# A third SBUF place for the down weights of a mixture-of-experts kernel, with router weights and list rows moved

## The chip, the cores and the metric

One core of one Trainium2 chip runs the whole kernel. The metric is the device time of one execution in microseconds (us); less is better. The kernel before took 942.89 us, the median of three runs (942.83 to 943.75). All times inside the kernel come from one profiled execution, and times of day in it are counted from its first instruction.

## The reference

The output mixes two branches by a sigmoid gate for each of 2048 tokens of 512 numbers. Branch A is a long causal convolution: a 4-tap convolution of `k` times `v`, then an FFT convolution with `ssm_k`, times `q`. Branch B is a mixture of eight experts with two chosen for each token:

```python
logits = einsum("bsd,de->bse", x, w_router)            # x = A_q, 8 experts
topk_idx = argsort(logits)[..., -2:]; gates = softmax(take(logits, topk_idx))
hg = silu(einsum("bsd,edf->bsef", x, w_gate))          # D = 512, F = 1376
hu = einsum("bsd,edf->bsef", x, w_up)
y  = einsum("bsef,efd->bsed", hg * hu, w_down)         # weighted by the gates and summed
g  = sigmoid((x * gate_w).sum(-1))
out = g * A(q, k, v) + (1 - g) * B(x)
```

## The kernel before

The kernel computes only the chosen tokens of each expert. It first finds the router's logits on TensorE (PE), ranks them, starts the fullest expert from a short list made for it alone, and makes the lists of all other experts (`routing`, `places`, `read_lists`) while the first expert runs. Then the experts r = 0 to 7 follow one another, each with up to 568 tokens.

**An expert.** F = 1376 is cut into eleven tiles ft = 0 to 10. For each, `up(ft)` loads the gate and up weights (`raw`, three places in SBUF, line 573) and the down weights (`rd`, line 623; for ft 2 of the first expert line 620), splits each into a high and a low fp32r half (`gh` on ScalarE, line 584, and `gl` on VectorE, line 590; `dh` on ScalarE, line 651, and `dl` on VectorE, line 653), and multiplies: the tokens are cut into two halves h, and for each h a product g and a product u of twelve matmuls (lines 200 to 202) fill a PSUM bank each, of three banks in turn. ScalarE makes `sg` = silu(g) (line 642), VectorE multiplies it by u (line 643), and the result is split into `hh` (ScalarE, 644) and `hl` (VectorE, 645). After ft 2, 5, 8 and 10 a group of tiles goes through the down product (`down`, tiles `yp`, gathered in `ya` on lines 678 and 680 or 701 and 704). The five places of `dh` and `dl` come free in groups of three when a down product is done, so the next three `rd` are wanted close together.

**Waits by place.** A load into a tile waits until the last reader of the tile that held its place before is done. With two places for `rd`, `rd` of ft 2 waits for `dl` of ft 0, and so on. The sync engine's queue (SP) issues loads strictly in order, so a load that waits holds back all loads behind it. Pools have named tags: `R3 = (3, 2, 2, 2)` on line 46 gives the number of places of `raw`, `gh`, `gl` and `rd`.

**The order of work.** Up to the first products of expert 0 the order is written by hand (`manual_schedule`). After that a list scheduler with a simulated clock places every instruction on its engine, so that a change of places can move instructions anywhere; each engine then runs its own list in order. Pieces of branch A are mixed in by `tick`: the spectra of `ssm_k` (`ks`, lines 279 and 293, with `kr` loaded on 224), the tap convolution `x_stage1` (`krow`, `v`, `tmp`, `acc`, lines 361 to 365), `x_stage2` and `y_stage`. The loads of the first expert that are not in the hand-written part wait for a gather to end (`behind_rows`, tied to the split of the last gathered rows on line 522).

**The parts that move.** `wr` (lines 153 and 154) holds the router weights and two small tables, 265 numbers per partition; only the start reads it. `late` holds two constant rows for the lists and a dummy column, loaded before expert 0; `idf` and `wsum` are working rows of `read_lists`, which runs once, at ft 5 of expert 0 (lines 913 to 918). All four lie in the pool `consts`, which lives as long as the kernel. The pool `route` ends when expert 0 has its rows. The tag "T" (three places of 512 numbers) serves `dD`, then `v` and `tmp` of `x_stage1`. `dD` is added to one row of `kr` by GpSimd (line 321).

Of the kernel before, what the change touches and what calls it, by code (L numbers as in the profile page):

```python
# [12 lines left out]
F32 = mybir.dt.float32  # L13
# [11 lines left out]
P = 128  # L25
S = 2048
D = 512
KT = D // P
F = 1376
E = 8  # L30
# [9 lines left out]
NT = MAIN + OVER  # L40
# [2 lines left out]
FT = [(i * P, min(P, F - i * P)) for i in range((F + P - 1) // P)]  # L43
SPREAD = 0.97
BW, EV, FX = (5, 3, 2)
R3 = (3, 2, 2, 2)
G0 = 5
TM = (5, 6, 7)
QA = 2
# [84 lines left out]
NLATE = P + 2 * NT + 1  # L134
# [4 lines left out]
def gated_mix(ctx: ExitStack, tc: tile.TileContext, a, out):  # L139
    nc = tc.nc  # L140
    sync, act, dve, pool, pe = nc.sync, nc.scalar, nc.vector, nc.gpsimd, nc.tensor

    dram = ctx.enter_context(tc.tile_pool(name="dram", bufs=1, space=DRAM))
    cp = ctx.enter_context(tc.tile_pool(name="consts", bufs=1))
# [5 lines left out]
    zd = dram.tile([P, 2, PL, D], F32, name="zd")  # L150
    lst = dram.tile([P, OVER, 2], I32, name="lst")

    wr = cp.tile([P, KT * 32 + 2 * E * E + E + 1], F32, name="wr")
    sync.dma_start(wr, a["wr"])
    ident = cp.tile([P, P], F32, name="ident")
    G = cp.tile([P, PL], F32, name="G")
    sidx = cp.tile([P, NT], I32, name="sidx")
# [4 lines left out]
    rc = cp.tile([P, NROW], F32, name="rc")  # L162
    colf = cp.tile([P, 2, PL], F32, name="colf")
    pay = cp.tile([P, 3, 2, PL], F32R, name="pay")
    idf = cp.tile([P, NT], F32, name="idf")
    wsum = cp.tile([P, NT], F32, name="wsum")
    late = cp.tile([P, 2 * NT + 1], F32, name="late")
    cols, spare, dummy = late[:, :NT], late[:, NT:2 * NT], late[:, 2 * NT:]
    row = cp.tile([P, 2, PL], F32, name="row")
    blk = cp.tile([P, OVER], I32, name="blk")  # L170
    nblk = cp.tile([P, 1], I32, name="nblk")
# [14 lines left out]
    def t2k(tag, bufs, name, dt=F32):  # L186
        return fp.tile([P, D], dt, tag=tag, bufs=bufs, name=name)
# [124 lines left out]
    def k_load(pl):  # L312
        n = k_order.index(pl)
        if n % 2 == 0:
            kr["two"] = two("B", f"kr{pl}")
        kr[pl] = half(kr["two"], n % 2)
        fetch(kr[pl], rows(a["ssk"], pl))
        if pl == 0:
            dD = t2k("T", 3, "dD")[0:1, :]
            sync.dma_start(dD, a["ssd"])  # L320
            pool.tensor_add(kr[0][0:1, :], kr[0][0:1, :], dD)
# [229 lines left out]
    def expert(r):  # L551
# [12 lines left out]
        def load(ft, eng=sync):  # L564
            fw = FT[ft][1]
            raw = wp.tile([P, 2 * KT * P], F32, tag="raw", bufs=R3[0], name=f"raw{r}_{ft}")
            n = 2 * KT * fw
# [11 lines left out]
        def split(ft, *engines, halves=(0, 1)):  # L579
            raw = st["raw", ft]  # L580
            n = raw.shape[1]
            if act in engines:
                st["gh", ft] = wp.tile([P, 2 * KT * P], F32R, tag="gh", bufs=R3[1], name=f"gh{r}_{ft}")[:, :n]
                anchor[f"gh {r} {ft}"] = act.activation(st["gh", ft], raw, AF.Copy).ins  # L584
            if dve in engines:
                if ("gl", ft) not in st:
                    st["gl", ft] = wp.tile([P, 2 * KT * P], F32R, tag="gl", bufs=R3[2], name=f"gl{r}_{ft}")[:, :n]
                c = slice(halves[0] * n // 2, (halves[-1] + 1) * n // 2)
# [26 lines left out]
        def load_down(ft, eng=sync):  # L615
            f0, fw = FT[ft]
            rd = wp.tile([P, D], F32, tag="rd", bufs=R3[3], name=f"rd{r}_{ft}")
            src = a["wd"][ds(st["e"], 1), f0:f0 + fw, :].rearrange("o f d -> (o f) d")
# [113 lines left out]
    wp = mp_ctx.enter_context(tc.tile_pool(name="moe_in", bufs=1))  # L732
    early = ExitStack()
    rp = early.enter_context(tc.tile_pool(name="route", bufs=1))
    io8 = rc[:, :8]
    capv = rc[:, 8:16]
    m_le = rc[:, 16:80].rearrange("p (a b) -> p a b", a=E)
# [35 lines left out]
    k_load(k_order[2])  # L773
    k_load(k_order[3])
    k_load(k_order[4])
    sync.dma_start(late, a["c_small"][:, P:NLATE])
    sync.dma_start(ident, a["c_small"][:, :P])
    for n in range(5, SEQ_N):
        k_load(k_order[n])
# [151 lines left out]
    for i in range(4):  # L931
        dve.tensor_tensor(hot0[:, i], u0[:, 4 * i:4 * i + 4].unsqueeze(1).to_broadcast([P, P, 4]), io4, op=ALU.is_equal)
        for j in range(4):
            n = 4 * i + j
# [200 lines left out]
    with tc.For_i(0, nb_v, 1) as b:  # L1135
        with tc.tile_pool(name="over", bufs=1) as op:
# [15 lines left out]
            for ft, (f0, fw) in enumerate(FT):  # L1152
                n = 2 * KT * fw
# [68 lines left out]
```

## Time and profile before

| | |
|---|---|
| median of three runs | 942.89 us (942.83 to 943.75) |
| the profiled execution | 943.57 us |
| its span, first to last instruction | 941.3 us |
| PE busy | 923.5 us, 98% of the span |
| VectorE (DVE) busy | 633.6 us, 67% |
| ScalarE (ACT) busy | 509.7 us, 54% |
| GpSimd (POOL) busy | 146.6 us, 16% |
| mean granted TensorE clock | 0.998 |
| DMA | 172.02 MB, mean 183 GB/s |

The profile counts an engine as busy while one of its instructions runs. A wait of one engine costs time only where PE, the engine that is nearly always busy, stands still for it, or at the two ends of the span. The views used below are the page, busy time by stretches, the list of who waited for whom, the DMA view of a stretch, and the order of instructions by time. In the last, each row has the start, the duration, engine, line, operation, the tile written and the tiles read, and in brackets the idle time just before with what ended it.

### The profile page before, as it was taken

To read this page: it belongs to the slowest core of one execution; us is meant where nothing else is said; L and a number is where in the kernel's file an instruction comes from. 1 tells how busy PE (TensorE), PEld (TensorE's weight loads), DVE (VectorE), ACT (ScalarE), POOL (GpSimd) and SP (SyncE) were. 2 spreads that over 40 slices of the span, in tenths; PEclk is the share of its full clock that TensorE was granted. 3 is DMA by queue.
4 is the path that set the end of the run, shared out by engine and by line. 5 is a ranking of instruction groups with operands and counts; after the bars stand their busy time and mean duration, and the time that the engine had idled before them with its cause. 6 is when DMAs were issued, how large, how long until landed. Compare 5 with 4: busy or idle time off the path is not lost. (4 is left out here: it accounts for less than half of the span.)

```text
span 941.3 us, 18097 instructions
## 1 busy us (share of the span) xinstructions
PE 923.5 (98%) x6957; PEld 830.0 (88%) x6957; DVE 633.6 (67%) x1131; ACT 509.7 (54%) x883; POOL 146.6 (16%) x137
## 2 busy tenths in 40 slices
PE   8999999999999999999999999999999999999996
PEld 4679999999999999978898889888887989889984
DVE  4796699999996557556767666765777645554541
ACT  4654334755456546478656876668766544234330
POOL 0320210300003020131101211013010310121012
PEclk9999999999999999999999999999999999999999
DMA  9895945754456463456445655456553786787233
GB/s 329 301 349 220 376 153 191 207 193 155 140 202 183 157 205 122 135 135 204 144 136 169 166 181 175 141 167 174 182 172 121 188 276 181 193 200 217 70 54 45
DMA packets 76378, 172.02 MB, mean 183 GB/s; under 512 B 8481, under 2 KB 9377, under 8 KB 76162
## 3 DMA queue, kind: packets, MB, share of 16 engines
q1 hardware_dynamic: 53490, 121.89, 38.4%
q0 software_dynamic: 12464, 29.02, 13.6%
q10 hardware_dynamic: 10336, 19.93, 5.8%
q8 instruction: 56, 0.92, 0.4%
q14 instruction: 32, 0.26, 0.1%
HBM read 127.24 MB, written 43.57 MB: 181 GB/s over the span
## 5 line engine op out<-in xcount | busy, mean ns | idle before, releaser
L200 PE MATMUL u<-xh,gh 128*128 128x256 f32 (+14 forms) x704 | 202.0, 287 | 2.5 <-ACT sg L642 2.5
L200 PE MATMUL g<-xh,gh 128*128 128x256 f32 (+17 forms) x696 | 200.8, 288 | 1.9 <-DVE sg L643 1.9
L202 PE MATMUL u<-xh,gl 128*128 128x256 f32 (+14 forms) x704 | 201.3, 286 | 0.0
L201 PE MATMUL u<-xl,gh 128*128 128x256 f32 (+14 forms) x704 | 201.1, 286 | 0.0
L202 PE MATMUL g<-xh,gl 128*128 128x256 f32 (+17 forms) x696 | 198.8, 286 | 0.0
L201 PE MATMUL g<-xl,gh 128*128 128x256 f32 (+17 forms) x696 | 198.6, 285 | 0.0
L200 PEld LDWEIGHTS g<-xh,gh 128*128 128x128 f32 (+1 forms) x696 | 129.5, 186 | 8.8 <-DVE sg L643 4.5
L200 PEld LDWEIGHTS u<-xh,gh 128*128 128x128 f32 (+1 forms) x704 | 130.9, 186 | 5.9 <-ACT sg L642 3.1
L201 PEld LDWEIGHTS u<-xl,gh 128*128 128x128 f32 (+1 forms) x704 | 130.9, 186 | 4.3 <-issue 4.1
L202 PEld LDWEIGHTS g<-xh,gl 128*128 128x128 f32 (+1 forms) x696 | 129.6, 186 | 4.3 <-issue 4.1
L202 PEld LDWEIGHTS u<-xh,gl 128*128 128x128 f32 (+1 forms) x704 | 131.1, 186 | 0.9 <-issue 0.8
L201 PEld LDWEIGHTS g<-xl,gh 128*128 128x128 f32 (+1 forms) x696 | 129.5, 186 | 2.4 <-issue 0.8
L642 ACT ACTIVATE sg<-g 128x256 f32<-128x256 f32 (+14 forms) x176 | 68.0, 387 | 111.9 <-PE g L202 110.6
L200 PE MATMUL yp<-hh,dh 128*128 128x264 f32 (+13 forms) x440 | 127.1, 290 | 0.0
L202 PE MATMUL yp<-hh,dl 128*128 128x264 f32 (+13 forms) x440 | 126.8, 289 | 0.0
L201 PE MATMUL yp<-hl,dh 128*128 128x264 f32 (+13 forms) x440 | 126.8, 288 | 0.0
L644 ACT ACTIVATE hh<-sg 128x256 fp32r<-128x256 f32 (+14 forms) x176 | 73.1, 418 | 98.6 <-DVE sg L643 98.0
L643 DVE TENSOR_TENSOR sg<-sg,u 128x256 f32<-128x256 f32 (+14 forms) x176 | 74.8, 426 | 72.2 <-PE u L202 70.7
L584 ACT ACTIVATE gh<-raw 128x1024 fp32r<-128x1024 f32 (+1 forms) x88 | 91.4, 1038 | 50.8 <-PE u L201 50.0
L590 DVE TENSOR_TENSOR gl<-raw,gh 128x1024 fp32r<-128x1024 f32 (+1 forms) x88 | 105.3, 1197 | 18.6 <-ACT gh L584 17.8
L645 DVE TENSOR_TENSOR hl<-sg,hh 128x256 fp32r<-128x256 f32 (+14 forms) x176 | 75.0, 429 | 24.8 <-ACT hh L644 24.5
L653 DVE TENSOR_TENSOR dl<-rd,dh 128x512 fp32r<-128x512 f32 (+1 forms) x88 | 59.5, 685 | 39.8 <-ACT dh L651 39.7
(283 smaller groups left out, 1549.6 us busy)
## 6 DMA issues: line engine op xcount, KB each, us to landing
raw<-in_wgu SPq DMA_DIRECT2D x80, 512.0 KB, 4.4
rd<-in_wd SPq DMA_DIRECT2D x80, 256.0 KB, 4.3
kl<-kd SPq DMA_DIRECT2D x16, 512.0 KB, 5.2
xl<-xd SPq DMA_DIRECT2D x32, 256.0 KB, 4.1
zd<-ze ACTq DMA_DIRECT2D x16, 512.0 KB, 3.9
zl<-zd SPq DMA_DIRECT2D x16, 512.0 KB, 5.9
out<-zt SPq DMA_DIRECT2D x21, 256.0 KB, 6.1
krow<-in_kpad SPq DMA_DIRECT2D x19, 256.0 KB, 5.5
```

What stands on the lines that cost most here:

```text
L200: pe.matmul(p, wh, hi, start=start, stop=False)
L201: pe.matmul(p, wh, lo, start=False, stop=False)
L202: return pe.matmul(p, wl, hi, start=False, stop=stop)
L584: anchor[f"gh {r} {ft}"] = act.activation(st["gh", ft], raw, AF.Copy).ins
L590: dve.tensor_sub(st["gl", ft][:, c], raw[:, c], st["gh", ft][:, c].bitcast(F32))
L642: act.activation(sg[:fw, :nn], pp[0][:fw, :nn], AF.Silu)
L643: dve.tensor_mul(sg[:fw, :nn], sg[:fw, :nn], pp[1][:fw, :nn])
L644: act.activation(hh[:fw, sl], sg[:fw, :nn], AF.Copy)
L645: dve.tensor_sub(hl[:fw, sl], sg[:fw, :nn], hh[:fw, sl].bitcast(F32))
L653: dve.tensor_sub(dl[:fw], rd[:fw], dh[:fw].bitcast(F32))
```

## The change

`rd` gets three places instead of two. Room for it comes from the pool `consts`: `wr` moves into the pool `route`, and `late`, `idf` and `wsum` become five slices of one tile that takes the first turn of the tag "T".

```diff
-R3 = (3, 2, 2, 2)
+R3 = (3, 2, 2, 3)
...
-    wr = cp.tile([P, KT * 32 + 2 * E * E + E + 1], F32, name="wr")
-    sync.dma_start(wr, a["wr"])
...
-    idf = cp.tile([P, NT], F32, name="idf")
-    wsum = cp.tile([P, NT], F32, name="wsum")
-    late = cp.tile([P, 2 * NT + 1], F32, name="late")
-    cols, spare, dummy = late[:, :NT], late[:, NT:2 * NT], late[:, 2 * NT:]
...
     rp = early.enter_context(tc.tile_pool(name="route", bufs=1))
+    wr = rp.tile([P, KT * 32 + 2 * E * E + E + 1], F32, name="wr")
+    sync.dma_start(wr, a["wr"])
+    late = t2k("T", 3, "late")
+    cols, spare, dummy, idf, wsum = (late[:, o:o + n] for o, n in ((0, NT), (NT, NT), (2 * NT, 1), (2 * NT + 1, NT), (3 * NT + 1, NT)))
...
-    sync.dma_start(late, a["c_small"][:, P:NLATE])
+    sync.dma_start(late[:, :2 * NT + 1], a["c_small"][:, P:NLATE])
```

Line numbers of the changed kernel are six lower from line 169 to 734 and two lower from line 735 on. What the scheduler makes of it is shown at three places. In the names, `dh_2` is `dh` of ft 2, `sg_1_0` is `sg` of ft 1, half 0; the last number of a name is the program's own count.

**First expert, ScalarE, ft 0 to 1.** Before:

```order
L642 ACTIVATE sg_0_1_598<-g_0_1_547 128x312
L584 ACTIVATE gh_2_722<-raw_2_483 128x1024
L644 ACTIVATE hh_0_578<-sg_0_0_580 128x256
L253 ACTIVATE ks11e<-ks11p 128x1024
L644 ACTIVATE hh_0_578<-sg_0_1_598 128x312
L254 DMA kd<-ks11e 256x1x512
L642 ACTIVATE sg_1_0_668<-g_1_0_642 128x256
L644 ACTIVATE hh_1_640<-sg_1_0_668 128x256
L651 ACTIVATE dh_2_792<-rd_2_790 128x512
L642 ACTIVATE sg_1_1_699<-g_1_1_673 128x312
L651 ACTIVATE dh_3_882<-rd_3_880 128x512
```

The same stretch after the change:

```order
L636 ACTIVATE sg_0_1_596<-g_0_1_545 128x312
L645 ACTIVATE dh_2_790<-rd_2_788 128x512
L578 ACTIVATE gh_2_720<-raw_2_481 128x1024
L638 ACTIVATE hh_0_576<-sg_0_0_578 128x256
L247 ACTIVATE ks11e<-ks11p 128x1024
L638 ACTIVATE hh_0_576<-sg_0_1_596 128x312
L248 DMA kd<-ks11e 256x1x512
L636 ACTIVATE sg_1_0_666<-g_1_0_640 128x256
L638 ACTIVATE hh_1_638<-sg_1_0_666 128x256
L636 ACTIVATE sg_1_1_697<-g_1_1_671 128x312
L645 ACTIVATE dh_3_880<-rd_3_878 128x512
```

`dh_2` moved up by seven rows, to stand ahead of `gh_2`, and `dh_3` now follows `sg_1_1` alone.

**First expert, ft 2 to 4, VectorE and PE.** VectorE before:

```order
L901 TENSOR_TENSOR hot<-row,rc 128x1024
L1058 TENSOR_TENSOR pay<-s_150,pay 128x32
L901 TENSOR_TENSOR hot<-row,rc 128x1024
L903 TENSOR_TENSOR sk<-colf,late 128x576
L643 TENSOR_TENSOR sg_2_1_785<-sg_2_1_785,u_2_1_772 128x312
L1044 CAST pay<-s_150 128x32
L903 TENSOR_TENSOR sk<-colf,late 128x576
L590 TENSOR_TENSOR gl_4_1003<-raw_4_999,gh_4_1001 128x1024
L906 TENSOR_TENSOR val<-sk,pay 128x8x72 x2
```

and after (`hot`, `sk` and `val` are the tables of the lists):

```order
L899 TENSOR_TENSOR hot<-row,rc 128x1024
L1056 TENSOR_TENSOR pay<-s_148,pay 128x32
L637 TENSOR_TENSOR sg_2_1_783<-sg_2_1_783,u_2_1_770 128x312
L1042 CAST pay<-s_148 128x32
L901 TENSOR_TENSOR sk<-colf,late 128x576
L899 TENSOR_TENSOR hot<-row,rc 128x1024
L901 TENSOR_TENSOR sk<-colf,late 128x576
L584 TENSOR_TENSOR gl_4_1001<-raw_4_997,gh_4_999 128x1024
```

PE at the same place, with the semaphores that a row waits for, before:

```order
L202 MATMUL u_3_0_831<-xh_433,gl_3_814 128x256
L293 MATMUL ks14p<-kr_997,c_90 128x512 [waits Activation_49]
L293 MATMUL ks14p<-kr_997,c_90 128x512
L200 MATMUL g_3_1_849<-xh_433,gh_3_812 128x312 [waits DVE_49]
L201 MATMUL g_3_1_849<-xl_434,gh_3_812 128x312
```

and after:

```order
L196 MATMUL u_3_0_829<-xh_431,gl_3_812 128x256
L287 MATMUL ks13p<-kr_995,c_85 128x512 [waits DMAHW0_49,PE_49]
L287 MATMUL ks13p<-kr_995,c_85 128x512
L194 MATMUL g_3_1_847<-xh_431,gh_3_810 128x312 [waits Activation_49]
L195 MATMUL g_3_1_847<-xl_432,gh_3_810 128x312
```

One `hot` and one `sk` moved behind the product `sg_2_1`; `ks13p` and `ks14p` each moved down by two products, and `g_3_1` takes another PSUM bank, so that it waits for ScalarE instead of VectorE. `g_4_0` now stands ahead of the first eight `list` matmuls, behind them and eighteen `yp` matmuls before.

**First expert, the second down product, VectorE.** Before:

```order
L680 TENSOR_TENSOR ya_1_909<-yp_1_1_0_1314,ya_1_909 128x256
L680 TENSOR_TENSOR ya_1_909<-yp_1_1_256_1325,ya_1_909 128x312
L680 TENSOR_TENSOR ya_2_932<-yp_1_2_0_1336,ya_2_932 128x256
L680 TENSOR_TENSOR ya_2_932<-yp_1_2_256_1347,ya_2_932 128x312
L680 TENSOR_TENSOR ya_3_955<-yp_1_3_0_1358,ya_3_955 128x256
L363 TENSOR_TENSOR tmp_1867<-krow_1774,sk 128x512
```

and after:

```order
L674 TENSOR_TENSOR ya_1_907<-yp_1_1_0_1312,ya_1_907 128x256
L357 TENSOR_TENSOR tmp_1865<-krow_1772,sk 128x512
L355 TENSOR_TENSOR acc_1864<-krow_1774,sk 128x512
L674 TENSOR_TENSOR ya_1_907<-yp_1_1_256_1323,ya_1_907 128x312
L358 TENSOR_TENSOR acc_1864<-acc_1864,tmp_1865 128x512
L357 TENSOR_TENSOR tmp_1865<-krow_1770,sk 128x512
```

The first `tmp`, which reads a loaded `krow`, moved ahead of four of the sums that empty the down product's banks.

## Rows read from the trace of the kernel before

**Rows 1.** The page, busy time of PE: us, share of the span, instructions.

```profile
PE 923.5 (98%) x6957; PEld 830.0 (88%) x6957; DVE 633.6 (67%) x1131; ACT 509.7 (54%) x883; POOL 146.6 (16%) x137
```

**Rows 2.** Busy time by stretches: the stretch, its length, then busy us and count of PE, PEld, DVE, ACT and POOL, granted clock, DMA share, GB/s.

```profile
30.00:70.00 40.00, 38.10 (x261) 32.00 (x259) 34.81 (x92) 22.87 (x39) 8.39 (x12) 1.00 0.92 330
...
110.00:400.00 290.00, 290.00 (x2234) 281.93 (x2233) 235.56 (x421) 153.96 (x274) 42.27 (x35) 1.00 0.55 175
```

**Rows 3.** Who PE waited for from 30 to 700 us: total us, times, longest.

```profile
PE u L200 <- ACT sg L642: 2.5, 3, 1.6
PE g L200 <- DVE sg L643: 1.9, 2, 1.2
```

**Rows 4.** Rows of PE in order of time (first ft 1 to 4 of the first expert, then the longest wait of a later one).

```profile
45.44 1.13 PE L293 MATMUL ks12p<-kr,c 64*128 64x512 f32 x4
...
51.98 0.41 PE L200 MATMUL g<-xh,gh 128*128 128x312 f32 x1 [0.65 <-DVE sg L643]
...
59.69 1.13 PE L293 MATMUL ks14p<-kr,c 64*128 64x512 f32 x4
...
62.07 0.42 PE L200 MATMUL g<-xh,gh 128*128 128x312 f32 x1 [1.25 <-DVE sg L643]
...
63.91 0.30 PE L200 MATMUL u<-xh,gh 128*128 128x312 f32 x1
...
65.72 1.13 PE L293 MATMUL ks15p<-kr,c 64*128 64x512 f32 x4
66.78 1.15 PE L908 MATMUL list<-val,hot 128*128 128x216 f32 x8
...
408.38 0.39 PE L200 MATMUL u<-xh,gh 128*128 128x264 f32 x1 [1.62 <-ACT sg L642]
```

**Rows 5.** Who waited for whom: the sync queue from 69 to 84 us.

```profile
SPq L623 <- DVE dl L653: 13.9, 1, 13.9
```

**Rows 6.** Who ScalarE waited for, whole span.

```profile
ACT dh L651 <- DMA rd<-in_wd: 17.1, 15, 2.9
```

**Rows 7.** Rows of ScalarE in order of time, first expert; the first is the split that ends the gather.

```profile
35.02 0.85 ACT L522 ACTIVATE xh<-xgp 128x512 fp32r<-128x512 f32 x2 [0.55 <-PE xgp L520]
...
38.03 0.43 ACT L642 ACTIVATE sg<-g 128x312 f32<-128x312 f32 x1
39.61 1.06 ACT L584 ACTIVATE gh<-raw 128x1024 fp32r<-128x1024 f32 x1 [1.15 <-PE u L201]
40.57 0.40 ACT L644 ACTIVATE hh<-sg 128x256 fp32r<-128x256 f32 x1
42.29 1.03 ACT L253 ACTIVATE ks11e<-ks11p 128x1024 f32<-128x1024 f32 x1 [1.32 <-DMA kd<-ks2e]
...
48.18 0.63 ACT L651 ACTIVATE dh<-rd 128x512 fp32r<-128x512 f32 x1 [2.89 <-DMA rd<-in_wd]
```

**Rows 8.** VectorE in order of time, ft 6 to 8 of the first expert.

```profile
95.17 0.23 DVE L918 TENSOR_TENSOR slot_w<-wsum,list 128x72 f32<-128x72 f32 x1
...
101.93 0.91 DVE L680 TENSOR_TENSOR ya<-yp,ya 128x312 f32<-128x312 f32 x2
...
110.57 0.69 DVE L363 TENSOR_TENSOR tmp<-krow,sk 128x512 f32<-128x512 f32 x1 [1.51 <-DMA krow<-in_kpad]
```

**Rows 9.** The sync queue's issues in order of time: the `rd` of ft 2 and of ft 3.

```profile
39.84 0.33 SPq L620 DMA_DIRECT2D rd<-in_wd  x1
40.66 0.87 SPq L623 DMA_DIRECT2D rd<-in_wd  x1
```

**Rows 10.** The DMA view of 40 to 42 us: q1 carries SP's loads, q0 those of POOL (packets, MB, share of 16 engines); then issues, KB each, median us to landing.

```profile
q0 software_dynamic: 227, 0.83, 101.8%
q1 hardware_dynamic: 5, 0.01, 1.5%
...
rd<-in_wd SPq DMA_DIRECT2D x2, 256.0 KB, 8.0
```

**Rows 11.** The page, DMA issues of the whole span: count, KB each, median us to landing.

```profile
rd<-in_wd SPq DMA_DIRECT2D x80, 256.0 KB, 4.3
```

**Rows 12.** Rows of VectorE in order of time, ft 1 to 3 of the first expert.

```profile
48.84 0.69 DVE L653 TENSOR_TENSOR dl<-rd,dh 128x512 fp32r<-128x512 f32 x1 [2.84 <-ACT dh L651]
...
51.46 0.47 DVE L643 TENSOR_TENSOR sg<-sg,u 128x312 f32<-128x312 f32 x1
...
58.50 1.32 DVE L1058 TENSOR_TENSOR pay<-s,pay 128x32 fp32r<-128x32 f32 x1
59.75 1.21 DVE L901 TENSOR_TENSOR hot<-row,rc 128x1024 fp32r<-128x1024 f32 x1
60.88 0.75 DVE L903 TENSOR_TENSOR sk<-colf,late 128x576 f32<-128x576 f32 x1
61.55 0.47 DVE L643 TENSOR_TENSOR sg<-sg,u 128x312 f32<-128x312 f32 x1
61.94 0.17 DVE L1044 CAST pay<-s 128x32 fp32r<-128x32 f32 x1
...
66.16 0.47 DVE L645 TENSOR_TENSOR hl<-sg,hh 128x312 fp32r<-128x312 f32 x1
```

**Rows 13.** GpSimd in order of time.

```profile
57.95 1.82 POOL L321 TENSOR_TENSOR kr<-kr,dD 1x512 f32<-1x512 f32 x1 [18.16 <-DMA kr<-in_ssk]
```

**Rows 14.** The sync queue in order of time: the loads of `krow`.

```profile
100.62 2.50 SPq L224 DMA_DIRECT2D krow<-in_kpad  x4
```

## The prediction

> **What bounds the kernel now.** I read the page first: PE is busy for 923.5 of the span's 941.3 us [rows 1], so 17.8 us is all that any change of waits can win. Next the busy time by stretches: from 110 to 400 us PE runs for all of 290.00 us at a granted clock of 1.00, while from 30 to 70 us it lacks 1.90 us, with VectorE at 34.81 of 40 us [rows 2]. The list of who waited for whom places the rest: between 30 and 700 us PE waits 4.4 us in all, 1.9 us in two waits for VectorE's `sg` and 2.5 us in three for ScalarE's [rows 3]. The two on VectorE are 0.65 us ahead of `g_2_1` at 51.98 and 1.25 us ahead of `g_3_1` at 62.07; of the others the longest, 1.62 us at 408.38, lies in a later expert [rows 4]. What is left of the 17.8 us is the start and the tail.
>
> The waits of queues for a place of `rd` are not among these. SP stands 13.9 us for one `dl` [rows 5] and ScalarE 17.1 us for `rd`, in 15 waits [rows 6], yet behind none of the later ones does PE stand still; the first, 2.89 us [rows 7], lies ahead of the wait at 51.98. The profiled execution took 943.57 us, 0.68 above the median; I make the sum on it and subtract 0.68 for the median. A measurement of this kernel can tell about 0.2%, 1.9 us, from no change: faster means below 941.0, slower above 944.8.
>
> **The change part by part.** *Moves that cost nothing.* The load of `wr` keeps its place as SP's first row. `late`, `idf` and `wsum` are the same instructions on other addresses; the one new wait is that of the first `tmp`, which takes their place and must come after `slot_w` at 95.17. Even when `tmp` moves from 110.57 up behind the first `ya` sum, to about 102.4 [rows 8], that is done 7 us earlier. If this cover were gone, `tmp` would be late by what is missing, and the `ya` sums behind it too.
>
> *Two loads of `rd`.* Before, ft 2's load waits for `dl` of ft 0 and is issued at 39.84, ft 3's at 40.66 [rows 9]. After, ft 2's waits only for the gather to end, 35.02 + 0.85 = 35.87 [rows 7]; ft 3's takes over the wait for `dl` of ft 0, about 39.9. The landing took 8.0 us here [rows 10] against a median of 4.3 [rows 11]. From 40 to 42 us the engines were full with POOL's queue, 101.8%, and SP's had 1.5% [rows 10]; so SP's loads stood behind the block of `kd` writes. For ft 2 that gives a landing between 36.0 + 4.3 = 40.3 and 36.0 + 8.0 = 44.0, and for ft 3 between 44.2 and 47.9 if its queue is served, or as late as 40.66 + 8.0 = 48.7 if not. I take 48.7 for ft 3, since it is issued into the block that those rows show.
>
> The Trainium skill, page "DMA: Bandwidth & Descriptors", section "Queues, rings and completion order", says that each DMA engine takes turns packet by packet between the queue rows that have work. By that rule SP's two loads would have shared those 2 us, ft 3's would land after about 4.3 us, the wait at 51.98 would go whole, and the time would be 941.3. The trace disagrees here: 1.5% is no half share [rows 10].
>
> *Term A, the wait at 51.98.* PE waits for the `sg` product of `g_1_1`, which VectorE starts at 51.46 behind two `dl`, at 48.84 and 50.45 (its duration is that of the first, 0.69) [rows 12]. After, `dl` of ft 2 is done earlier (-0.69) and `dh` of ft 3 follows `sg_1_1` alone, but its load lands some 0.5 us later than the 48.2 at which ScalarE got ft 2's before [rows 7]. The product starts about 0.3 earlier. **A = -0.3**, bounds -0.65 and 0.
>
> *Term B, the wait at 62.07.* VectorE starts the product `sg_2_1` at 61.55, behind one `hot` and one `sk` from 59.75 on (1.80 us) and a `pay` of 1.32 us; a cast of the same 128x32 takes 0.17 [rows 12]. That `pay` ran while GpSimd added `dD` from 57.95 on, for 1.82 us [rows 13]; I put the 1.15 us between the two to that. After, `hot` and `sk` stand behind the product and GpSimd's addition behind three `kd` writes. With A's 0.3 the product starts at 61.55 - 0.3 - 1.80 - 1.15 = 58.3. `g_3_1` no longer needs it, as it takes the bank of `g_3_0`, and the next that does, `u_3_1`, comes at about 61.2. **B = -1.25**, bounds -1.25 and 0.
>
> *Term C, a new wait.* `g_4_0` now stands ahead of the first eight `list` matmuls, and 18 `yp` no longer do. `g_3_1` starts at 62.07 - 1.25 - 0.3 - 1.06 (one `ks` less ahead of it) = 59.5. Up to `list` come 1.84 + 1.81 + 1.06 us as between 62.07 and 66.78 [rows 4], and `g_4_0`, 1.84 x 256/312 = 1.51: PE is there at 65.7. VectorE ends `sg_2_1` at 58.8 and has the 4.22 us from 61.94 to 66.16 [rows 12], the 1.80 moved behind and one row of 0.47 to do until `val` is ready: 65.3; or 66.4, if GpSimd's addition now costs 1.15 there. The wait is 0 to 0.7. **C = +0.3**, bounds 0 and 1.5 (both, and one 0.75 us `sk` more ahead of it).
>
> *SP's 13.9 us.* Gone: ft 7's `rd` then waits for `dl` of ft 4. What stood behind it on SP (clears of the output, a `raw`, then `sk` and `krow`) goes earlier, `krow` from 100.62 [rows 14] to some 90 to 92. I cost this at nothing, since PE did not wait behind it; what it frees early may collide, which is a rival below. The order around 400 us is that of before, so the 1.62 us at 408.38 stay.
>
> **Sum**: -0.3 - 1.25 + 0.3 = -1.25 us; 943.57 - 1.25 = 942.3 on the profiled execution, **941.6** on the median's scale. With all bounds on one side it runs from 941.0 (A and B whole, C nothing) to 943.1 (B whole, A nothing, C 1.5).
>
> **The rivals.** *VectorE is the bound* from 30 to 70 us, and the wait only moves: it does the same instructions, at 87% busy [rows 2]. Then `list` takes over what A and B gave: 942.9. For it speaks that the first expert's lists are a chain on VectorE; against it, that the 1.15 us of the slow `pay` are no work.
>
> *Both waits go, and more*: the load lands early, GpSimd's addition meets nothing, A = -0.65, B = -1.25, C = 0, and one of the two smaller waits on ScalarE goes with the new order ((2.5 - 1.62)/2 = 0.45 [rows 3, 4]): 942.9 - 1.9 - 0.45 = 940.5; with both of them 940.1.
>
> *Slower, by `dh` of ft 2.* It now stands ahead of `gh_2`, `hh` and `ks11e`, and ScalarE stops there until its load lands. The four take 0.63 + 1.06 + 0.40 + 1.03 = 3.1 us [rows 7], and PE needs `ks11e` out of its bank for `ks12p` at 45.44 [rows 4]. It decides from a landing at 42.3; at 44.0 it takes back 1.7, about what A and B gave. Landing as late as before, 48.2, it costs 5.9: 942.9 + 5.9 - 1.9 = 946.9. Against it: the issue is 3.9 us earlier, ahead of most of the `kd` block.
>
> *Slower, by `tmp`.* It now stands on VectorE ahead of the sums that free the down product's banks. If `krow` comes no earlier than before, when it ended a wait at 110.57 [rows 8], VectorE stops from 102.4 for 8.2 us. PE has three banks and up products meanwhile; I take 3.3 us of the 0 to 8.2: 942.9 - 1.25 + 3.3 = 944.9. It decides from a landing at 102.4. Against it: SP loses its 13.9 us.
>
> **How the numbers follow.** Forecast 0.50; VectorE as the bound 0.17; both waits and more 0.20; `dh` 0.06; `tmp` 0.07. Faster: the 0.20 and the lowest 0.08 of the forecast, 0.28. Slower: `dh` and most of `tmp`, 0.12. Same: the remaining 0.60. The range goes from 940.1, the end of the faster case, to 944.1, the forecast's 943.1 and 1 us of a partial stop at `dh` or `tmp`.
>
> **What would show it.** Right: SP's wait of 13.9 us is gone and ScalarE's sum on `rd` falls well below 17.1, with a first wait of 2 to 6 us at `dh` of ft 2 ahead of `gh_2`; PE's wait at 62 is gone, that at 52 is 0 to 0.4; a wait on `val` at `list` near 65 is under 0.8; 1.62 us near 408 stay; the clock is 1.00. Wrong: PE waits at `ks12p` for `ks11e`, or for a bank of `yp` near 103 with VectorE waiting for `krow`; or a new wait of over 1 us in a later expert, where I found none in the order. If the time falls by more than 3 us, the tail or the start has moved, of which I expect nothing.

## The result: slower, by something behind the first expert

The changed kernel takes 949.33 us (median of 22 runs, 945.61 to 962.34) against 942.85 us for the kernel before, measured between them (22 runs, 941.07 to 951.31). The ratio is 1.0069, with a 95% interval of 1.0045 to 1.0092: 0.7% slower. Three of its 22 runs, at 960 us and more, count in the median and not in the ratio. The forecast was 941.6 us, and the range ended at 944.1. A second series gave 950.92 us against 941.82, a ratio of 1.0097 [1.0082, 1.0113].

The profiled execution took 947.01 us, with a span of 945.1 us. First the page's busy times after the change, and then the two stretches of [rows 2] with the same columns:

```profile
PE 926.2 (98%) x6957; PEld 830.5 (88%) x6957; DVE 632.2 (67%) x1131; ACT 504.7 (53%) x883; POOL 149.4 (16%) x137
```

```profile
30.00:70.00 40.00, 39.33 (x276) 34.01 (x275) 35.73 (x94) 22.82 (x41) 12.02 (x13) 1.00 0.93 336
110.00:400.00 290.00, 288.19 (x2200) 277.56 (x2199) 227.97 (x410) 148.38 (x269) 41.74 (x34) 1.00 0.54 166
```

From 30 to 70 us PE lacks 0.67 us in place of 1.90: this is the gain that was forecast. From 110 to 400 us, where PE had run without a gap, it lacks 1.81 us and does 34 matmuls less. VectorE is *less* busy there, 228 us in place of 236: it stands still, and not because it has less to do. Who PE waited for from 30 to 700 us, to be held against [rows 3] (total us, times, longest):

```profile
PE u L194 <- ACT sg L636: 3.8, 4, 1.8
PE yp L194 <- DVE ya L674: 1.1, 3, 0.7
PE ks12p L287 <- ACT ks11e L247: 0.4, 1, 0.4
PE yp L195 <- DVE hl L639: 0.4, 1, 0.4
PE list L906 <- DVE val L904: 0.2, 1, 0.2
PE g L194 <- DVE sg L637: 0.2, 1, 0.2
```

The two waits on `sg` of VectorE in the first expert are gone, 1.9 us. New are the waits for `ya` and `hl` (all between 150 and 260 us), and the group on ScalarE's `sg` has grown by 1.3 us. What VectorE itself waited for from 110 to 300 us, first before, then after the change:

```profile
DVE acc L361 <- DMA krow<-in_kpad: 2.2, 3, 1.2
...
DVE tmp L363 <- DMA krow<-in_kpad: 1.5, 1, 1.5
```

```profile
DVE acc L355 <- DMA krow<-in_kpad: 9.9, 10, 1.7
```

This is the trail: the loads of `krow`, which the change doesn't touch, come too late ten times in place of four. The waits are inferred from who ended them; the experiments test whether they are the loss.

### The profile page after: what moved, and what is told of

Its sections match the earlier page's. It is cut to its first block, busy times and chain, and to the rows that moved or that the text cites. A ratio compares the mean times of both kernels' runs of the same rounds, so it can differ in the third digit from the quotient of the medians.

```text
span 945.1 us, 18100 instructions
## 1 busy us (share of the span) xinstructions
PE 926.2 (98%) x6957; PEld 830.5 (88%) x6957; DVE 632.2 (67%) x1131; ACT 504.7 (53%) x883; POOL 149.4 (16%) x137
## 5 line engine op out<-in xcount | busy, mean ns | idle before, releaser
L505 POOL DMA_INDIRECT xg<-in_q,gidx x37 | 40.0, 1081 | 305.4 <-PE xgp L514 230.6
```

The costliest lines, as they stand in the source:

```text
L505: anchor["pool"] = pool.indirect_dma_start(out=xg[:w], out_offset=None, in_=a["q"], in_offset=bass.IndirectOffsetOnAxis(ap=gidx[:w, col:co ...
```

## The experiments

Each was timed in rounds with the kernel before; that kernel's medians were 941.82 us (first four), 942.34 (next four) and 942.34 (last four). Behind each time stands its ratio to that kernel with the 95% interval; it is not the quotient of the two medians and can differ from it by 0.2%. L is the theory that the new order makes `krow` late, S that the moved tiles at the start are to blame, O that any new order costs.

**The changed kernel again**, with no edit.

> The changed kernel once more, for a second trace of it. Theory L (the loads of krow now stand behind rd on the sync queue and come too late for VectorE between 110 and 330 us): VectorE waits about 10 us for krow between 110 and 300 us, against 3.7 us before, PE loses 2 to 4 us in that stretch, and the time is 946 to 950 us. Theory S (the start: the moved router weights make the first logits late and the clock falls, 0.91 and 0.50 granted between 6 and 10 us in the first trace): the first product g of expert 0 starts over 1 us later than the 31.71 us of before, and PE loses nothing between 110 and 330 us.

950.92 us, 1.0097 [1.0082, 1.0113]. This execution (span 948.2 us) shows the loss at its plainest. VectorE's and PE's waits from 110 to 300 us:

```profile
DVE acc L355 <- DMA krow<-in_kpad: 13.3, 10, 3.7
```

```profile
PE yp L194 <- DVE ya L674: 2.4, 3, 1.4
PE yp L195 <- DVE hl L639: 2.2, 2, 1.8
PE u L194 <- ACT sg L636: 0.2, 1, 0.2
```

The longest, followed through three engines in order of time: the sync queue, VectorE, then PE.

```profile
170.32 0.33 SPq L567 DMA_DIRECT2D raw<-in_wgu  x1
170.86 1.44 SPq L617 DMA_DIRECT2D rd<-in_wd  x1
172.34 0.51 SPq L218 DMA_DIRECT2D krow<-in_kpad  x1
```

```profile
177.41 0.44 DVE L637 TENSOR_TENSOR sg<-sg,u 128x276 f32<-128x276 f32 x1
181.55 0.69 DVE L355 TENSOR_TENSOR acc<-krow,sk 128x512 f32<-128x512 f32 x1 [3.70 <-DMA krow<-in_kpad]
...
183.60 1.22 DVE L584 TENSOR_TENSOR gl<-raw,gh 128x1024 fp32r<-128x1024 f32 x1
184.74 0.44 DVE L639 TENSOR_TENSOR hl<-sg,hh 128x276 fp32r<-128x276 f32 x1
```

```profile
185.23 0.39 PE L195 MATMUL yp<-hl,dh 128*128 128x276 f32 x1 [1.81 <-DVE hl L639]
```

`raw`, `rd` and `krow` leave in one burst, the moment `raw` is let go; `krow`, last of the three, is there 9.2 us after its issue. VectorE has reached `acc` after 5.5 us, stands for 3.70 us with `gl` and `hl` queued behind, and PE, which needs `hl`, stands for 1.81. All five of PE's waits on VectorE in this stretch, 4.6 of the 4.8 us, begin within 4.3 us behind a stop of VectorE for `krow`, and four of the five are in the first trace too, at the same instructions.

The order of this burst is not new, though: in the kernel before the same three loads left at 169.18, 169.71 and 170.62, `krow` was there after 6.9 us, and VectorE waited 0.77. In the first trace of the changed kernel it was there after 6.9 us as well, with a wait of 1.35. So the longest stop is for the most part a late landing of this one execution. Over rows 4 to 15 of the convolution `krow` stands directly behind an `rd` eight times in the changed kernel and five times in the kernel before.

Theory S fails here: the clock at the start was 1.00 in this execution, and the first product began at 31.49 us (31.71 before).

**The moves without the third place.**

```diff
-R3 = (3, 2, 2, 3)
+R3 = (3, 2, 2, 2)
```

> Two places for rd as before, but wr, late, idf and wsum at their new places; the order on all engines is that of before. Theory L: the order is all, so the time is that of before, 942.9 +- 1 us, and VectorE waits under 4 us for krow. Theory S: the new places do it, the time is 945 us or more with a mean clock of 0.997 or less.

942.31 us, 1.0019 [1.0000, 1.0039]; VectorE waits 2.8 us for `krow` and PE not at all from 110 to 300 us. The moved tiles cost next to nothing, and since the order is that of before, this is a second trace of it. In it PE's wait near 62 us is absent and that near 52 is 0.24 us; its span is 940.0 us.

**The third place for one load alone.** In this and four later runs a load waits as with two places where a condition holds (`dls` lists the `dl` instructions):

```diff
+        def as_two(i, ft):
+            if ((r, ft) != (0, 2)) and len(dls) > 1:
+                tc.add_manual_dep(i, dls[-2].name, ...)
```

> The changed kernel, but every rd load other than that of ft 2 of expert 0 waits for the dl two tiles back, as with two places; on the sync queue krow stays ahead of rd as before. Theory L: the gain of the first expert without the loss behind it: PE's two waits of 1.9 us near 52 and 62 us are gone but for about 0.6, VectorE waits under 5 us for krow between 110 and 300 us, the time is 941 to 942.5 us. Theory S: 946 us or more. Rival O (any new order of the list scheduler costs some us, whatever it moves): 944 to 948 us, with waits of PE in places that krow does not explain.

943.60 us, 1.0010 [0.9988, 1.0032]: between L and O. `krow` cost VectorE 7.7 us and PE waited 1.2 us between 130 and 330 us; in the first expert PE waited 0.9 us at `ks12p` for `ks11e` and 0.8 us for VectorE's `sg`, nearly what it had waited there before. The large loss is gone, but not the lateness.

**Three places, with `krow` at high priority**, so that the queue reads `raw`, `krow`, `rd`.

```diff
+            with tc.high_priority() if r > 0 else nullcontext():
                 krows[r] = load("A", 6, f"krow{r + 3}", ...)
```

> The changed kernel with three places, but the loads of krow of rows 1 to 15 at high priority, so that each goes ahead of the rd that it stood behind; the first expert keeps the changed order. Theory L: VectorE's waits for krow between 110 and 300 us fall from 9.9 to under 4 us, PE's waits of 1.9 us there go, and the time is 941 to 943.5 us. Theory S and rival O: as the changed kernel, 946 to 950 us.

944.38 us, 1.0021 [1.0003, 1.0040]: 6.5 of the 9.1 us come back. VectorE waits 5.7 us for `krow` and the time is 0.9 us above L's range, both more than L said, but PE has no wait from 130 to 330 us. S falls, and so does O as a full account.

**The third place in experts 1 and 2 alone.**

```diff
-            if ((r, ft) != (0, 2)) and len(dls) > 1:
+            if (r < 1 or r > 2) and len(dls) > 1:
```

> The third place serves experts 1 and 2 alone: in expert 0 and from expert 3 on each rd load also waits for the dl two tiles back, as with two places. The order up to 110 us is that of before; from there krow stands behind rd on the sync queue as in the changed kernel (R d K). Theory L (krow too late): PE waits 2 to 5 us between 130 and 330 us, VectorE over 8 us for krow, PE's wait near 530 stays at 0.6, and the time is 946 to 950 us. Rival E (the loss needs the first expert's new order, which lets VectorE run ahead): 941 to 943 us and under 4 us for krow.

943.81 us, 1.0007 [0.9986, 1.0028]. L in its first form misses: `krow` stands behind `rd` as in the changed kernel, VectorE waits 7.2 us for it, PE once, 1.8 us, directly behind the `krow` stop of 2.15 us, yet the time hardly moves. Rival E misses too, in the wait (it allowed 4 us) and in the time (it ended at 943). Whether the full loss needs the first expert's new order as well stays open.

**The third place from expert 3 on.**

```diff
+            if (r < 3) and len(dls) > 1:
```

> The third place serves experts 3 to 7 alone; the order up to about 400 us is that of before. Theory L: nothing is lost between 110 and 330 us; the only loss is PE's wait for sg near 530, 0.63 us before and 1.84 us in the changed kernel, so 941.5 to 943.5 us. Rival O (any new order costs some us): 944 us or more, with new waits of PE behind 400 us.

944.66 us, 1.0030 [1.0005, 1.0054]. The time lies above L's range and in that of O, but the trace shows one grown wait and no others: a second, smaller loss, at one place. PE there in the kernel before, then here, then its stretches here (columns as in [rows 2]):

```profile
529.73 0.39 PE L200 MATMUL u<-xh,gh 128*128 128x264 f32 x1 [0.63 <-ACT sg L642]
```

```profile
523.84 0.28 PE L195 MATMUL g<-xl,gh 128*128 128x260 f32 x1
523.97 0.28 PE L196 MATMUL g<-xh,gl 128*128 128x260 f32 x1
526.09 0.39 PE L194 MATMUL u<-xh,gh 128*128 128x260 f32 x1 [1.84 <-ACT sg L644]
...
527.56 0.42 PE L196 MATMUL u<-xh,gl 128*128 128x260 f32 x1
```

```profile
520.00:525.00 5.00, 4.25 (x34) 4.04 (x34) 2.36 (x4) 4.95 (x7) 3.75 (x3) 1.00 0.94 215
525.00:530.00 5.00, 3.91 (x20) 3.91 (x21) 3.97 (x5) 2.84 (x6) 0.00 (x0) 0.66 1.08 287
530.00:535.00 5.00, 5.00 (x43) 4.44 (x46) 2.98 (x6) 1.22 (x4) 0.00 (x0) 0.99 0.44 148
```

The wait of 0.63 us is 1.84 here, as in all runs with a third place in experts 3 and 4. ScalarE shows why, first with the order of before (the moves alone), then here:

```profile
523.76 0.39 ACT L636 ACTIVATE sg<-g 128x264 f32<-128x264 f32 x1
524.18 2.13 ACT L432 ACTIVATE sw<-y 32x1024 f32<-32x1024 f32 x2
526.32 1.06 ACT L433 ACTIVATE sw<-y 32x1024 f32<-32x1024 f32 x1
```

```profile
522.43 2.12 ACT L433 ACTIVATE sw<-y 32x1024 f32<-32x1024 f32 x2
524.57 1.06 ACT L434 ACTIVATE sw<-y 32x1024 f32<-32x1024 f32 x1
525.65 0.67 ACT L644 ACTIVATE sg<-g 128x264 f32<-128x264 f32 x2
```

The `sg` that PE needs stood ahead of three `sw` copies and now stands behind them. In this execution PE also ran part of the next 5 us at the lower level of its clock, 1.2 GHz (0.66 granted over the 5 us, matmuls of 0.42 us in place of 0.28). From 526.09 on the next 24 matmuls took 4.5 us, where they took 3.0 in the changed kernel: 1.5 us more, 2.7 us in all with the longer wait.

**`krow` behind `rd` with two places**: the suspected cause without the change.

```diff
-R3 = (3, 2, 2, 3)
+R3 = (3, 2, 2, 2)
...
+            with tc.issue_after(rds[-1]) if r > 0 else nullcontext():
                 krows[r] = load("A", 6, f"krow{r + 3}", ...)
```

> Two places for rd as before, with the other moves, but each krow load of rows 1 to 15 must be issued behind the last rd in program order (d K instead of K d): the suspected cause without the third place. Theory L: VectorE waits over 10 us for krow between 110 and 330 us, PE loses 4 us or more there, and the time is 947 us or more. If the position of krow isn't the cause, it stays at 941.5 to 943.5 us.

942.48 us, 1.0008 [0.9979, 1.0037]: L's first form falls. All twelve later `krow` stand behind `rd`, and VectorE waits 0.9 us. So I took from each trace, for the rows 4 to 15 of the convolution, the time from the issue of `krow` to the moment when VectorE reaches the `acc` that needs it, and set the wait beside it:

```
                          issue to reached   VectorE's wait   PE's waits
                          (mean of 12, us)   for krow in acc  130 to 330 us
the change, first trace         4.5                9.9             1.9
the change, again               4.4               13.3             4.8
third place, experts 1 and 2    4.4                7.2             1.8
third place, krow first         4.8                5.7             0
third place, one load           5.0                7.7             1.2
two places, moves only          5.0                2.8             0
two places, krow late           5.5                0.9             0.3
```

It is not the place in the queue by itself. The list scheduler sets both lists by its own clock; when it puts `krow` last in a burst and `acc` 4.4 us behind, nothing is left for a landing of up to 9 us. With two places and `krow` late it had also moved `acc` back. This is theory L2. The table alone does not prove it, since a shorter time from issue does not always go with longer waits: it is 4.4 us with the third place in experts 1 and 2, where little is lost, and 5.0 with one load, where VectorE waits 7.7. How long a load takes to land counts as well, and that differs from one execution to the next.

**`krow` first, in the kernel before**: the control of the high priority.

```diff
+            with tc.high_priority() if r > 0 else nullcontext():
                 krows[r] = load("A", 6, f"krow{r + 3}", ...)
```

> The kernel before with krow of rows 1 to 15 at high priority: the control for the experiment that put krow first with three places. Theory L: krow already stood ahead of most rd, so VectorE's waits of about 3 us and the time change little: 941 to 943 us. If high priority alone saves 4 us or more, it takes some other loss away, and the recovery with three places says nothing about rd.

942.59 us, 1.0009 [0.9977, 1.0041]: no change, so the priority alone gains nothing.

**The newest row last.** The burst stays on the sync queue; only VectorE's need moves.

```diff
-        dve.tensor_mul(acc, krow(pl), sk[:, 0])
-        for tap in range(1, TAPS):
+        dve.tensor_mul(acc, krow(pl - TAPS + 1), sk[:, TAPS - 1])
+        for tap in reversed(range(TAPS - 1)):
             dve.tensor_mul(tmp, krow(pl - tap), sk[:, tap])
```

> The changed kernel, but the tap convolution takes its oldest row first and its newest krow last, so that VectorE needs each loaded krow some 4 us later; on the sync queue the loads still stand as R d K. Theory L2 (not krow's place in the queue by itself, but the time from its issue to VectorE's first need of it, some 4.5 us against a landing of 5 to 9 behind raw and rd): VectorE's waits for krow fall from 13.3 to under 5 us, PE's waits between 130 and 330 us from 5 to under 1 us, and the time falls from 950.9 to 942 to 945 us, what is left being the wait near 530. Rival V (VectorE is behind for other reasons, its waits for krow only fill idle time): no change, 948 us or more.

943.74 us, 1.0002 [0.9977, 1.0028], against 1.0097 for the changed kernel. By the medians 7.7 of the 9.1 us come back. VectorE's waits for `krow` from 85 to 320 us fall to 2.3 us (12.6 in the changed kernel's first trace, 15.9 in its second), PE has none from 110 to 300 us, and only the wait near 530 stays at 1.84:

```profile
DVE acc L355 <- DMA krow<-in_kpad: 2.1, 2, 1.4
...
DVE tmp L357 <- DMA krow<-in_kpad: 0.2, 1, 0.2
```

The need moved by more than the 4 us that were meant: the product that reads the new row now comes 18.9 us behind its load on the mean of rows 4 to 15 (4.4 before), since the scheduler could also start most of these rows ahead of their load. The same burst is now harmless, as the sync queue shows:

```profile
168.71 0.33 SPq L567 DMA_DIRECT2D raw<-in_wgu  x1
169.24 0.52 SPq L617 DMA_DIRECT2D rd<-in_wd  x1
169.80 0.43 SPq L218 DMA_DIRECT2D krow<-in_kpad  x1
```

**The newest row last, in the kernel before.**

```diff
-        for tap in range(1, TAPS):
+        for tap in reversed(range(TAPS - 1)):
```

> The kernel before with the same order of taps: the control. Theory L2: it waits only about 3 us for krow and PE loses nothing by it, so the time stays within 1.5 us of 942. Rival V or a gain of the tap order by itself: more than 3 us either way.

942.19 us, 1.0015 [0.9982, 1.0047]: the order of taps by itself gives nothing. V falls, and L2 holds in so far: VectorE's waits for `krow` do cost PE time, and with more time between load and need they are gone.

**`krow` first, third place in experts 0 to 2 alone.**

```diff
+            with tc.high_priority() if r > 0 else nullcontext():
...
+            if (r > 2) and len(dls) > 1:
```

> Three places with krow at high priority as in the experiment that put krow first (944.4 us), but from expert 3 on with the wait of two places. Theory: what was left of the loss there is PE's wait for sg near 530 (1.84 us instead of 0.63, and at times a lower clock behind it), which comes with the third place in experts 3 to 4. Then the wait is 0.6 us again and the time 942 to 943.3 us; if the rest lies elsewhere it stays at 944 to 945.

943.45 us, 1.0012 [1.0000, 1.0024]. The waits on ScalarE's `sg` sum to 2.3 us (3.7 in the changed kernel from 300 to 700 us), so the wait near 530 is small again; the time missed the 943.3 of the first case by a hair, and this execution kept 7.4 us of VectorE waiting for `krow` and 1.2 us of PE at `ks12p`.

**The newest row last, third place in experts 0 to 2 alone**: both losses taken away.

```diff
+        for tap in reversed(range(TAPS - 1)):
...
+            if (r > 2) and len(dls) > 1:
```

> Three places with the newest krow last, and the wait of two places from expert 3 on: both losses taken away. Theory L2 with the wait near 530: 941 to 942.5 us, not slower than before. If a third loss exists: 943.5 us or more.

941.46 us, 0.9990 [0.9978, 1.0002]. Who PE waited for from 110 to 935 us:

```profile
PE u L194 <- ACT sg L644: 2.3, 3, 1.4
```

Nothing is left of the change's loss. Nor is there a gain that can be told from no change: the interval holds 1. (From expert 3 on this kernel waits as with two places, so it is not the whole change.)

## Why the prediction was wrong

**The first expert: right in mechanism, wrong in what it was worth.** ft 2's `rd` was issued at 36.01, and ScalarE had it at 43.23, inside 40.3 to 44.0:

```profile
43.23 0.63 ACT L645 ACTIVATE dh<-rd 128x512 fp32r<-128x512 f32 x1 [4.65 <-DMA rd<-in_wd]
```

That is past the 42.3 of the `dh` rival, by whose rule it would cost 0.9 us; the price was the 0.43 us at `ks12p`. The `sg` product of `g_1_1` started at 51.07 (51.2 forecast), that of `g_2_1` at 58.21 (58.3), and the wait at `list` was 0.24 us at 65.91 (0.3 at 65.7):

```profile
51.07 0.47 DVE L637 TENSOR_TENSOR sg<-sg,u 128x312 f32<-128x312 f32 x1
...
58.11 0.19 DVE L1056 TENSOR_TENSOR pay<-s,pay 128x32 fp32r<-128x32 f32 x1
58.21 0.47 DVE L637 TENSOR_TENSOR sg<-sg,u 128x312 f32<-128x312 f32 x1
```

ft 3's `rd`, issued at 39.97, was ready when ScalarE came to it at 48.20, earlier than my 48.7 by an amount that this trace does not show; in the run with the newest row last ScalarE did stop for it, until 48.09, 8.5 us after its issue. The DMA engines of the changed kernel, from 42 to 43 us and from 46 to 47 (columns as in [rows 10]):

```profile
q0 software_dynamic: 110, 0.41, 99.9%
q1 hardware_dynamic: 16, 0.02, 5.6%
```

```profile
q1 hardware_dynamic: 55, 0.21, 51.8%
q0 software_dynamic: 53, 0.19, 48.1%
```

The hole of [rows 10] is there again: 2 to 4 us after their issue SP's loads move almost nothing, and the 0.06 MB of SP's queue from 42 to 44 us are not the 256 KB of a load that lands at 44.2. Once they run, the two queues share the engines about evenly, as the Trainium skill says (page "DMA: Bandwidth & Descriptors", section "Queues, rings and completion order": an engine takes turns between the queues that have work). So the rule holds for the later part, and a landing near 48 for the whole; whether POOL's block or a slow start makes the hole, no run here tells. A was whole all the same, but only in part by what I had reckoned with: the product of `g_1_1` came 0.39 us earlier, and PE, held up at `ks12p`, came to `g_2_1` 0.46 us later (51.79 in place of 51.98 - 0.65 = 51.33).

So A was whole (-0.65), B whole (-1.25), C +0.24, `dh` +0.43: -1.23 us, where the sum said -1.25. That the two are so near is luck: A and `dh`, each off by about 0.4, cancel. (The sum's upper end of 943.1 is also too low by its own bounds: with A and B at nothing and C at 1.5 it is 944.4.)

And what A and B take away is not in every execution. B was a mishap. With the order of before, the slow `pay` of 1.32 us [rows 12] and the wait of 1.25 us behind it [rows 4] came back in only one of six further traces (two places, newest row last); in the other five `pay` took 0.18 to 0.20 us and the wait was 0 to 0.44 us; near 52 the six show 0 to 0.26 us in place of 0.65. From 36 to 110 us PE waits 0.2 to 1.9 us in the seven traces with the order of before, 0.7 on the mean, and 0.3 to 1.5 us in the six with the changed order, 0.7 on the mean too. So by these traces the first expert gains nothing. The profiled execution stood 0.68 us above the median of three runs, and 0.7 to 1.8 above the later ones. What the change took away, the kernel before mostly did not pay.

**The step that failed is "I cost this at nothing, since PE did not wait behind it"**, on what SP's 13.9 us set free. SP's wait for `dl` did shrink, to 6.9 us, and `krow` went out at 92.72 (90 to 92 forecast). But the later lists were rearranged as well: `rd`, free of its own wait, went out together with `raw`, and `krow` directly behind an `rd` eight times of twelve (five before). In place of nothing the runs showed 1.9 us of PE's waiting from 110 to 300 us in the first trace and 4.8 in the second, behind 9.9 and 13.3 us of VectorE's for `krow`, and 1.2 us more near 530. The row that spoke against me was in my own table: from 110 to 400 us VectorE was busy 235.56 of 290 us [rows 2], and before 300 us far more, 85.96 of the 90 us from 110 to 200 (columns as in [rows 2]):

```profile
110.00:200.00 90.00, 90.00 (x680) 87.72 (x679) 85.96 (x153) 48.40 (x90) 16.76 (x10) 1.00 0.63 197
```

I read PE's 290.00 of 290.00 as safety, where VectorE behind it had 4% to spare. The order of the sync queue, which shows `raw`, `rd`, `krow`, entered the prediction for the first expert only. "A new wait of over 1 us in a later expert, where I found none in the order" was the condition for being wrong, and the `sg` behind three `sw` near 530 stood in ScalarE's order too.

**The rival on `tmp`** named the right loads at the wrong place: VectorE did stop for `krow` behind the first sums, 2.69 us, but PE did not.

```profile
103.19 0.69 DVE L357 TENSOR_TENSOR tmp<-krow,sk 128x512 f32<-128x512 f32 x1 [2.69 <-DMA krow<-in_kpad]
```

The rival on VectorE as the bound had the right engine, one expert too early. And `dh <- rd`, the wait that the change removes, fell from 17.1 us [rows 6] to 5.0: the change does what it says, and the wait was hidden, as the prediction had it.

**The balance.** Between the second trace of the changed kernel (948.2 us) and that of the moves alone (940.0 us) lie 8.2 us. PE's waits from 110 to 300 us make 4.8, the longer wait near 530 1.2, `ks12p` and one late `kr` 0.7; 0.2 near 52, which the moves alone had, is gone. A stop also cost 0.16 us beyond the idle time that its row shows (523.97 to 526.09 above is 2.12 us from start to start, where 0.12 is usual and 1.84 is shown), which gives an estimate of 1.1 us for seven stops more. That makes 7.6; the rest is not accounted for.

**What stays open.** Why landings differ so from run to run (the changed kernel's runs spread over 17 us) was not traced; the table above has one execution for each kernel. All kernels but that of the moves alone have lists of their own, so no run changes `krow`'s lateness and nothing else. No run made `krow` late on purpose and lost time by it: the one that tried did not make it late. And each of the seven edited kernels with a third place, whatever was edited, came out at 941.5 to 944.7 us, so that the list of the changed kernel may be an unlucky one among many.

## What to carry to other kernels

A freed wait that nobody stood behind is not free of charge if a scheduler re-plans from it: read the new order of every queue as far as it differs, above all where an engine with a few per cent to spare feeds the bound one, and set issue-to-need times against the landings that the trace shows for a load at the end of a burst. Before a gain is booked on a stall, ask whether it is in every execution; a row seven times slower than its like is a sign that two engines met there, and they may meet at another row next time. And a load's lateness can be mended at its reader: taking the newest operand last took away 6 to 9 us of loss (ratio 1.0002 in place of 1.0069 and 1.0097) where the queue kept its burst.

## What the runs showed of the hardware

GpSimd's addition of `dD` and VectorE met once in all fourteen traces: the VectorE row that was running when the addition ended was the slow one, and rows of 128x32 ended 0.04 to 0.06 us behind the addition, the longer `hl` 0.34 to 0.35. In the kernel before this was `pay`, which ended at 58.50 + 1.32 = 59.82 [rows 12], 0.05 us behind the addition (57.95 + 1.82 = 59.77 [rows 13]). With the moves alone it was the cast behind the product `sg_2_1`, and in the changed kernel `hl`; first the two rows of the moves alone, then of the changed kernel:

```profile
58.46 2.38 POOL L315 TENSOR_TENSOR kr<-kr,dD 1x512 f32<-1x512 f32 x1 [19.04 <-DMA kd<-ks12e]
60.02 0.86 DVE L1042 CAST pay<-s 128x32 fp32r<-128x32 f32 x1
```

```profile
59.27 4.24 POOL L315 TENSOR_TENSOR kr<-kr,dD 1x512 f32<-1x512 f32 x1 [0.48 <-issue]
62.62 1.23 DVE L639 TENSOR_TENSOR hl<-sg,hh 128x312 fp32r<-128x312 f32 x1
```

With the order of before `pay` paid in two traces (1.32 us) and the cast in the other five (0.86 to 0.88 us in place of 0.17); with the changed order `hl` paid in all six (1.22 to 1.24 us in place of 0.47 [rows 12]); in the run with the third place for one load it was the cast, 1.26 us. So the collision did not go away; it met a row ahead of the product in the profiled execution, a row behind it in most others, and after the change a row ahead of `val`, where term C had left room for it. The addition itself took 1.41 to 4.73 us. No run here moves the addition alone or shows why the two hold each other up.

A stop of PE of the same length, 1.84 us at the same place, left the granted clock at 1.00 in four traces (the changed kernel's two, `krow` first, newest row last) and was followed by 0.66 over the next 5 us in one (third place from expert 3 on). At the start of the changed kernel's first trace a wait of 1.16 us for the first logits was followed by a granted clock of 0.91 (6 to 8 us), 0.50 (8 to 10 us) and 0.73 (10 to 12 us): the lower level, 1.2 GHz, for part of this time. The first product of the first expert still started only 0.13 us later than before (31.84 against 31.71): the wait of 1.19 us for gathered rows that stood ahead of it in the kernel before was gone.
